# Attention and a routed FFN on one core: the first batch's start reordered, gate halves and threshold moved, and the end behind the last output rearranged

## The chip, the cores and the metric

The kernel runs on one core of a Trainium2 chip. A core has TensorE (PE, with its weight load PEld), VectorE (DVE), ScalarE (ACT), GpSimd (POOL) and SyncE (SP), each with a queue of its own that it works off in order. SBUF is the working memory, PSUM holds what TensorE writes. The metric is the time of one execution on the device, in microseconds; lower is better.

## The reference

For each of eight batches of 3136 tokens (z 64 wide, u and v 256 wide):

```
scores = z z^T / 3136;  attn = max(scores, 0)^2;  x = u * (attn v)
s = x . w_gate;  the 128 tokens with the largest s are chosen
x[chosen] += sigmoid(s) * (relu(x[chosen] w1) w2)        # w1 256 x 1024, w2 1024 x 256
```

The result is x in float32. In the matmuls of attention and FFN each operand is split into a high part (rounded to fp32r) and a low part (the rest), and three of the four products are summed.

## The kernel before

The tokens of a batch are cut into seven chunks of columns (five of 512, one of 256, one of 320; `WHOLE` is 5, `NCH` is 7) and 24 blocks of 128 rows and a half one. A slot is one pair of row blocks against one chunk; a chunk has 13 slots (`SLOTS`), the last with the half block (`n == 1`). Slots are written out in order by the loop at the end, and everything is emitted by hand in that order (`manual_schedule`), so every engine works in the order of the program text.

In a slot k, `mix` (L487) issues PE's matmuls for the slot (`acc`, L517): the high parts, then the low parts. In between, at `turn`, it calls `more_scores(k + LEAD)`, which issues the score matmuls (`sc`, L411) of three slots later and, on ACT, relu (L421) and the square that is rounded to the high part (L422). `settle_scores` then squares on DVE (`a`, L432) and calls `low` (L436), which transposes squares for later use by other chunks (L447), stores them to DRAM, and takes the low part (`lo`, L478) on DVE or POOL, whichever `busy` says has less to do. Scores are symmetric, so later chunks fetch stored squares (`fetch`, `fetch_own`) instead of computing them. A bank of PSUM for scores comes free when DVE has squared it.

`start` (L1199) does the first loads, splits and scores: ten idle matmuls on zeros (`warm`), z and v of the first batch, the split of z into `ZH` and `ZL` and the first chunk's moving operand `Z` (`bring_z`, upper half from ACT, lower from DVE). v is staged in two `vst` buffers, four transfers to a buffer (`stage_v`, L274), and split by `prep_v` (L119 and L120). The same two buffers take the FFN's weights in batch 0 (`load_weight`), which are split into `wh`, `wl` and stored to DRAM (`keep_weight`), and a chunk's own squares (`fetch_own`).

At the end of a chunk, `finish` (L555) multiplies by u (`ut`, L562), transposes x on DVE (`turn`, L573) and stores it (four transfers of 256-byte pieces, L580), and sums the gate. The routing of a batch (`route`: a search for the threshold by eight rounds of count and total, then masks, columns, places, one-hot picks) and its FFN (`expert`: gather by POOL, `hidden`, `turn_h`, `back` to y, scatter by POOL) are lists of tasks, each with PE's operations and a post for the other engines; the loop hands them out to slots of the next batch. In the eighth batch there is no next one: routing starts in its fourth chunk over the first three chunks' tokens (`LATE` is 4), with the gate's 48 columns of runs split into halves by two DVE instructions (`halve`, L653 and L654) to fill more rows, and each later chunk is merged into the choice (`merge`: spread of old scores, counts on DVE, pick, find). A planner in the loop decides by sums of its own (`clock`, `dve_at`, `room`, `ready`) when such a task may go into a slot.

Two FFNs, of batches 5 and 6, are kept (`HELD`, `put_off`) and run behind the last output, beside the last merge (lists f0, s0 of one and f1, s1 of the other; `f` holds the hidden matmuls, the transposes and the first 16 y matmuls, `s` the low parts and the last 8 y and the scatter). Then comes the last batch's own FFN.

```
        late, seen, *rest, find = rest
        run([*rest[: n - 1], f0[0], rest[n - 1], late, seen])
        run([*blend(rest[n:], [*f0[1:], *f1[:2]]), find])
        rest = [*first[:2], *f1[2:], *s0, *s1[:2], *first[3:], *ffn, more[0], *s1[2:], *more[1:]]
```

In the last line `first` is number, gather, nothing, weigh (gate of the chosen, sigmoid) and turn (transpose of the gathered rows and their split).

Of the kernel before, what the change touches and what calls it, by code (L numbers as in the profile page):

```python
# [84 lines left out]
def attention_then_routed_ffn(ctx: ExitStack, tc: tile.TileContext, zt, ut, v, wg, w1, w2, cst, cst16, keys, outs, at, cap):  # L85
# [146 lines left out]
    def prep_z(b, i, of=None):  # L232
# [6 lines left out]
        on = nc.gpsimd.tensor_tensor if b else None  # L239
# [28 lines left out]
    def stage_v(b, g, queue=nc.sync):  # L268

        st = stage.tile([P, GT, D], F32, name="vst", tag="vst")  # L270
        if g < NJ // GT:
            for f in range(GT):
                src = v[b, g * CH + f * P : g * CH + (f + 1) * P, :].rearrange("(t a) d -> a t d", a=Q)
                queue.dma_start(st[f * Q : (f + 1) * Q], src)  # L274
# [5 lines left out]
    def prep_v(b, g, on=None):  # L280
# [10 lines left out]
        if not on and b == 0 and busy["pool"] + 1.3 > busy["dve"] + 0.6:  # L291
            lo_on, took = nc.vector, {"act": 0.6, "dve": 0.6}
# [106 lines left out]
    def scores(k):  # L399
# [9 lines left out]
        for q, j in enumerate(js):  # L409
            for z, start in ((ZH, True), (ZL, False)):  # L410
                nc.tensor.matmul(ps[:, q], z[:, j * P : (j + 1) * P], mov, start=start, stop=not start)  # L411
# [24 lines left out]
    def low(k, a, hi, pieces, square):  # L436
# [5 lines left out]
        rows = slice(0, P) if n == 2 else slice(64, P)  # L442
        if turns(k):
# [36 lines left out]
        else:  # L480
            nc.vector.tensor_tensor(hi[rows], a[rows], hi[rows].bitcast(F32), op=ALU.subtract)
            spend(dve=0.05 + 0.001 * w)
# [4 lines left out]
    def mix(k, beside, between):  # L487
# [24 lines left out]
        turn = (6 if b or c else 3) if first else 4 if last or len(slots[min(k + 1, len(slots) - 1)][2]) == 1 else 8  # L512
# [42 lines left out]
    def finish(b, c):  # L555
# [13 lines left out]
        x = tail.tile([P, CH // Q, NK, Q], F32, name="x", tag="x", bufs=1)[:, :NB]  # L569
# [23 lines left out]

        turns = [lambda h=h: turn(h) for h in range(NK)]
        if scored:
            return [([], turns), ([], [None, add])]
        spread, seen = scores_of(b, c, xT)
        return [(spread, turns), ([], [lambda q=q: seen(q) for q in range(2)])]
# [41 lines left out]
    def route(b):  # L640
# [10 lines left out]
        def halve():  # L651
            whole = gate[b][:, : R // 2]
            nc.vector.tensor_scalar(gate[b][:, R // 2 : R], whole, consts["half"][:, 1:2], None, op0=ALU.mult)  # L653
            nc.vector.tensor_scalar(whole, whole, consts["half"][:, 0:1], None, op0=ALU.mult)  # L654
            spend(dve=0.4)
# [44 lines left out]
        def settle(rd):  # L700
# [7 lines left out]
            base = moe.tile([TP, 1], I32, name="base", tag="base", bufs=2)[:R]  # L708
            if rd == 0:
# [16 lines left out]
        def masks():  # L726
            t = st["base"].bitcast(F32)
            mk = moe.tile([TP, 2 * NT], BF16, name="mk", tag="mk")[:R]
            nc.vector.tensor_scalar(mk[:, :NT], G, t, None, op0=ALU.is_gt)
            nc.vector.tensor_scalar(mk[:, NT:], G, t, None, op0=ALU.is_equal)  # L730
# [218 lines left out]
    def expert(b, st, n):  # L949
# [49 lines left out]
        def bank(name, e):  # L999
            if not roomy:  # L1000
                return misc_bank(name)
            if name == "h" or (not lent and name == "y"):
                return ps_s.tile([P, 2, 512], F32, name=name, tag="sc")[:, 0]
            if lent:
                return ps_a.tile([P, 512], F32, name=name, tag="acc")
            if e == 0:
                st["pair"] = ps_s.tile([P, 2, 512], F32, name=name, tag="sc")
            return st["pair"][:, e]

        def hidden(e, i):  # L1010
            if i == 0:
                st["h", e] = bank("h", e)
# [15 lines left out]
        def turn_h(e, f):  # L1028
            if f == 0:
                st["hT", e] = bank("hT", e)  # L1030
# [22 lines left out]
        def back(i):  # L1053
            if i == 0:
                st["ps"] = bank("y", 0)
# [24 lines left out]
        if roomy:  # L1080
            return first, hid, [tur[0], dif[0], tur[1], dif[1], (to_y, scatter)]
# [17 lines left out]
    for b in range(B):  # L1099
# [18 lines left out]
        for g in range(NJ // 2 + 1):  # L1118
            k = k0 - 10 + 3 * g // 2 if b else max(1, g - 2)
            if b or g > 1:  # L1120
# [78 lines left out]
    def start():  # L1199
        warm(10)  # L1200
# [28 lines left out]
    for k, (b, c, js, is_old) in enumerate(slots):  # L1229
# [8 lines left out]
        if len(js) == 2:  # L1238
            if near and (k % SLOTS or c <= NCH - late if late else k % SLOTS % 3 == 2):
                tasks.append(near.popleft())  # L1240
            if far and far[0] is None and not near and not tasks and not (late and c > NCH - late):
                far.popleft()
                rested = k + 2
            if late and c >= NCH - late:

                left = sum(took_by(i) for i in range(k, k - k % SLOTS + SLOTS))
                room = clock + min(took, left - 3.5)
                asked = 0
                while far and rested <= k and asked < 2 and dve_at + 0.5 * asked < room:
                    if far[0] is None:  # L1250
                        if near:
# [3 lines left out]
                    if far[0][0] and (asked or ready > clock + took):  # L1255
# [16 lines left out]
        if k + 1 < len(slots) and len(slots[k + 1][2]) == 1:  # L1272
# [36 lines left out]
    if merged(B - 1):  # L1309
# [3 lines left out]
        late, seen, *rest, find = rest  # L1313
        n = len(rest) - len(last_merge) + 2
        run([*rest[: n - 1], f0[0], rest[n - 1], late, seen])
        run([*blend(rest[n:], [*f0[1:], *f1[:2]]), find])
        order.enter_context(tc.manual_schedule())
        rest = [*first[:2], *f1[2:], *s0, *s1[:2], *first[3:], *ffn, more[0], *s1[2:], *more[1:]]
# [29 lines left out]
```

## Time and profile before

| | us |
|---|---|
| median of 3 runs (2145.92 to 2148.81) | 2146.33 |
| profiled execution | 2144.29 |
| its span, first to last instruction | 2142.5 |
| TensorE busy | 2105.7 (98%) |
| VectorE busy | 1519.2 (71%) |
| GpSimd busy | 1347.3 (63%) |
| ScalarE busy | 1219.9 (57%) |
| mean granted TensorE clock | 0.995 |

The rows below come from one profiled execution; its time is the span and 1.8 us around it. A view of waits says who waited for whom: us in total, number of waits, longest. A timeline gives start, duration, engine, line, operation, written and read tiles, shape, and in brackets how long the engine had stood idle before and what ended it. Durations of matmuls overlap, so a group's duration holds the last one's drain.

### The profile page before, as it was taken

The page shows a single profiled execution, that of the slowest core. Times are in us where ns is not written, and L with a number is a line of the kernel's source. Part 1 is how long each engine was busy: PE and PEld are TensorE (multiplying, and loading weights), DVE is VectorE, ACT ScalarE, POOL GpSimd, SP SyncE. Part 2 cuts the span into 40 slices and gives each one's busy share as a digit, 9 for nine tenths or more (in the row PEclk, how much of TensorE's full clock was granted, in tenths as well). Part 3 has the DMA queues.
Part 4 walks back from the last instruction along what each step waited for, and adds up shares of the span by engine and source line. Part 5 has one row for each costly group of instructions (what it writes and reads, how often), then busy time and mean ns, then how long its engine had stood idle before and what let it go on. Part 6 is the DMA issues. An engine that isn't in the chain of part 4 may idle for free.

```text
span 2142.5 us, 31762 instructions
## 1 busy us (share of the span) xinstructions
PE 2105.7 (98%) x10575; PEld 1762.2 (82%) x10575; DVE 1519.2 (71%) x2305; ACT 1219.9 (57%) x1488; POOL 1347.3 (63%) x706
## 2 busy tenths in 40 slices
PE   8999999999999999999999999999999999999998
PEld 6778988889888898888988889888888889887787
DVE  7756677765777668776677757776678766877774
ACT  6555476545765457654665546655466554765343
POOL 5765576664766558665586556765576665766543
PEclk9999999999999999999999999999999999999999
DMA  6789666787667876778767777678867687756742
GB/s 173 210 256 228 192 200 176 191 235 217 182 190 191 228 219 189 198 192 224 218 188 207 188 217 225 184 188 193 248 188 207 175 209 190 205 165 184 194 141 79
DMA packets 432948, 422.27 MB, mean 197 GB/s; under 512 B 150160, under 2 KB 341136, under 8 KB 429200
## 3 DMA queue, kind: packets, MB, share of 16 engines
q1 hardware_dynamic: 431440, 417.63, 70.8%
q0 software_dynamic: 768, 2.10, 0.3%
q8 instruction: 83, 1.36, 0.3%
q10 hardware_dynamic: 576, 0.52, 0.1%
q14 instruction: 81, 0.66, 0.1%
HBM read 235.31 MB, written 172.23 MB: 190 GB/s over the span
## 4 chain that ended last, share of the span: by engine, by line
PE 84%; DMA 4%; DVE 3%; issue 3%; ACT 3%; POOL 2%; SPq 1%; POOLq 0%; DVEq 0%; ACTq 0%
PE acc L517 68%; PE sc L411 13%; POOL lo L478 2%; ACT a L421 1%; ACT hi L422 1%; DVE a L432 1%; DMA squares_narrow<-aT 1%; DMA qk<-squares 1%; PE h L1015 1%; PE y L1059 1%; DMA vst<-in_w 1%; DMA ut<-in_ut 0%; SPq L580 0%; DVE beats L871 0%; DVE ut L562 0%
## 5 line engine op out<-in xcount | busy, mean ns | idle before, releaser
L517 PE MATMUL acc<-hi,V 128*128 128x512 f32 (+2 forms) x5376 | 1235.2, 367 | 3.7 <-DVE V L120 2.4
L478 POOL TENSOR_TENSOR lo<-a,hi 128x1024 fp32r<-128x1024 f32 (+2 forms) x327 | 756.4, 2315 | 609.4 <-DVE a L432 503.3
L517 PEld LDWEIGHTS acc<-hi,V 128*128 128x128 f32 x5376 | 935.9, 189 | 169.5 <-DVE ut L562 5.1
L517 PE MATMUL acc<-lo,V 128*128 128x512 f32 (+2 forms) x2688 | 671.6, 366 | 8.4 <-POOL lo L478 8.3
L421 ACT ACTIVATE a<-sc 128x1024 f32<-128x1024 f32 (+4 forms) x408 | 363.2, 890 | 537.4 <-PE sc L411 418.0
L517 PEld LDWEIGHTS acc<-lo,V 128*128 128x128 f32 x2688 | 474.5, 189 | 96.1 <-POOL lo L478 14.2
L432 DVE TENSOR_TENSOR a<-sc,a 128x1024 f32<-128x1024 f32 (+3 forms) x334 | 338.4, 1013 | 278.7 <-ACT hi L422 247.3
L391 ACT CAST hi<-qk 128x1024 fp32r<-128x1024 f32 (+2 forms) x320 | 275.4, 863 | 254.1 <-PE acc L517 200.4
L447 DVE STREAM_TRANSPOSE aT<-a 128x512 f32<-128x512 f32 (+1 forms) x520 | 341.2, 691 | 85.4 <-ACT a L427 53.6
L422 ACT ACTIVATE hi<-a 128x1024 fp32r<-128x1024 f32 (+4 forms) x408 | 377.5, 925 | 17.4 <-PE acc L517 0.2
L478 DVE TENSOR_TENSOR lo<-qk,hi 128x1024 fp32r<-128x1024 f32 (+2 forms) x219 | 292.4, 1342 | 81.6 <-ACT hi L391 76.1
L411 PE MATMUL sc<-Z,ZH 128*128 128x512 f32 (+2 forms) x760 | 283.0, 376 | 4.8 <-DVE Z L256 3.1
L411 PE MATMUL sc<-Z,ZL 128*128 128x512 f32 (+2 forms) x760 | 283.5, 377 | 0.4 <-DVE ZL L120 0.4
L478 POOL TENSOR_TENSOR lo<-qk,hi 128x1024 fp32r<-128x1024 f32 (+2 forms) x101 | 194.1, 1924 | 64.0 <-ACT hi L391 48.5
L411 PEld LDWEIGHTS sc<-Z,ZH 128*128 128x128 f32 x760 | 143.8, 189 | 33.9 <-ACT ZH L119 3.9
L411 PEld LDWEIGHTS sc<-Z,ZL 128*128 128x128 f32 x760 | 143.6, 189 | 26.6 <-DVE ZL L120 0.8
L120 POOL TENSOR_TENSOR V<-vst,V 128x512 fp32r<-128x512 f32 x89 | 122.4, 1380 | 48.0 <-ACT V L119 44.8
L582 POOL TENSOR_TENSOR ut<-x,w_run 128x1024 f32<-128x1024 f32 (+2 forms) x52 | 127.2, 2447 | 25.9 <-DVE x L573 23.9
L119 ACT CAST V<-vst 128x512 fp32r<-128x512 f32 x95 | 57.7, 608 | 39.9 <-DMA vst<-in_v 39.9
L427 ACT ACTIVATE a<-a 128x1024 f32<-128x1024 f32 x74 | 78.5, 1061 | 2.3
L120 POOL TENSOR_TENSOR ZL<-zst,ZH 128x512 fp32r<-128x512 f32 (+2 forms) x56 | 77.9, 1395 | 3.0 <-ACT ZH L119 2.8
L562 DVE SCALAR_TENSOR_TENSOR ut<-acc,ut 128x512 f32<-128x512 f32 (+2 forms) x112 | 64.0, 612 | 19.4 <-PE acc L517 16.4
(148 smaller groups left out, 1045.7 us busy)
## 6 DMA issues: line engine op xcount, KB each, us to landing
squares<-aT SPq DMA_DIRECT2D x160, 512.0 KB, 3.5
qk<-squares SPq DMA_DIRECT2D x320, 256.0 KB, 5.9
squares_narrow<-aT SPq DMA_DIRECT2D x320, 128.0 KB, 3.4
qk<-squares_narrow SPq DMA_DIRECT2D x80, 512.0 KB, 5.0
vst<-in_v SPq DMA_DIRECT2D x188, 128.0 KB, 3.3
ut<-in_ut SPq DMA_DIRECT2D x40, 512.0 KB, 5.4
out<-x SPq DMA_DIRECT2D x160, 128.0 KB, 3.3
squares_own<-aT SPq DMA_DIRECT2D x39, 256.0 KB, 2.1
```

The source lines that it names most:

```text
L120: (lo_on or nc.vector.tensor_tensor)(lo, src, hi.bitcast(F32), op=ALU.subtract)
L391: nc.scalar.copy(by(hi), src)
L411: nc.tensor.matmul(ps[:, q], z[:, j * P : (j + 1) * P], mov, start=start, stop=not start)
L421: nc.scalar.activation(a, ps[:, :n], AF.Relu)
L422: nc.scalar.activation(pieces[0][0](hi), pieces[0][1], AF.Square)
L427: nc.scalar.activation(a, a, AF.Square)
L432: square = lambda: nc.vector.tensor_tensor(a[rows], ps[rows, :n], a[rows], op=ALU.mult)
L447: nc.vector.transpose(to, a[rows, q].rearrange("p (m t a) -> p m t a", t=GT, a=Q))
L478: on.tensor_tensor(view(lo), src, view(hi).bitcast(F32), op=ALU.subtract)
L517: nc.tensor.matmul(ac[h], w, mov, start=first and h not in started, stop=stop)
L562: nc.vector.scalar_tensor_tensor(xT[:, h, :w], acc[b, c][h], SCALE * SCALE, xT[:, h, :w], op0=ALU.mult, op1=ALU.mult)
L582: nc.gpsimd.tensor_tensor(wx, runs, consts["wg_run"].rearrange("p (o r) -> p o r", o=1).broadcast_to([P, NB, RUN]), op=ALU.mult,)
```

## The change

- `start`: twelve idle matmuls instead of ten; the second z load goes ahead of v; two of v's first four transfers go from ACT's queue to SP's; ZL's subtraction for the first block comes behind the lower half of `Z`; both first squares are done before any low part; the split of V's third pair moves here. In the first two score pairs the high parts' matmuls come first.
- `low`: a half block's subtraction (`hi`, L481) comes ahead of its transposes. `mix`: in the first slot of batches 1 to 7, scores are issued after four matmuls, not six.
- Weights of the FFN: loads and splits move from slots 19 to 33 to the second halves of the second and third chunk (loads at 8, 9, 11, 13 of the chunk, splits at 10, 12, 14, 16), and each stored weight follows at slot 17 from that chunk's start.
- `halve` goes to ACT. In the last round of the search the threshold is written to PSUM, and the masks are tensor_tensor with it broadcast, no longer tensor_scalar.
- The planner of the eighth batch: the routing's first task waits a slot more, tasks with matmuls stay out of the first two slots of later chunks, and the last chunk may be filled to 1.5 of its end instead of 3.5.
- Behind the last output x is turned by PE (`flip`, two transposes into a PSUM bank for each 128 tokens), copied by ACT and stored row by row, three transfers. The old scores' spread goes ahead; one kept FFN stands beside the last merge; of the other, the hidden matmuls stand behind the find, the transposes behind the turn, and y in pieces between the last FFN's steps; weigh comes behind the turn. The last y is summed in another order, and banks of PSUM are taken from other pools.

```diff
     def start():
-        warm(10)
+        warm(12)
...
-        stage_v(0, 0, nc.scalar)
         stage_z(0, 1, (WHOLE - 1) * CH, CH)
+        stage_v(0, 0, (nc.scalar, nc.scalar, nc.sync, nc.sync))
...
-        prep_z(0, 0)
+        low_parts = []
+        prep_z(0, 0, on=lambda *x, **how: low_parts.append(lambda: nc.vector.tensor_tensor(*x, **how)))
         bring_z(0, 0)
+        for fn in low_parts:
+            fn()
...
-        settle_scores()
         more_scores(1)
+        square_scores()
         prep_v(0, 1)
         settle_scores()
         prep_z(0, 2, 1)
+        prep_v(0, 2)
...
+        todo = [(q, j, z) for q, j in enumerate(js) for z in (ZH, ZL)]
+        if k < 2:
+            todo.sort(key=lambda x: x[2] is ZL)
...
-        turn = (6 if b or c else 3) if first else 4 if last or ...
+        turn = (6 if c else 4 if b else 3) if first else 4 if last or ...
...
+        def flip(i):
+            h, i = i % NK, i // NK
+            o, n = groups_of(w)[i]
+            if h == 0:
+                flipped.append(ps_a.tile([P, 512], F32, name="flip", tag="acc"))
+            nc.tensor.transpose(flipped[i][:n, h * P : (h + 1) * P], xT[:, h, o : o + n], consts["ident"])
...
-            nc.vector.tensor_scalar(gate[b][:, R // 2 : R], whole, consts["half"][:, 1:2], None, op0=ALU.mult)
-            nc.vector.tensor_scalar(whole, whole, consts["half"][:, 0:1], None, op0=ALU.mult)
+            nc.scalar.mul(gate[b][:, R // 2 : R], whole, consts["half"][:, 1:2])
+            nc.scalar.mul(whole, whole, consts["half"][:, 0:1])
...
+            if rd == last:
+                base = st["ps"][:R, 64:65].bitcast(I32)
...
-            nc.vector.tensor_scalar(mk[:, NT:], G, t, None, op0=ALU.is_equal)
+            nc.vector.tensor_tensor(mk[:, NT:], G, t, op=ALU.is_equal)
...
-        at_slots(SLOTS + 6 + 2 * i, load, use, 0.6)
+        k = (1 + i // 4) * SLOTS
+        loads.append((k + (8, 9, 11, 13)[i % 4], load))
+        at_slot(k + 10 + i % 4 * 2, use, 0.6)
...
-        at_slot(SLOTS + 6 + 8 * i - 1, lambda i=i: keep_weight(i))
+        at_slot(i * SLOTS + 17, lambda i=i: keep_weight(i))
...
-                room = clock + min(took, left - 3.5)
+                room = clock + min(took, left - (3.5 if c < NCH - 1 else 1.5))
...
-                        if near:
+                        if near or (tasks and c == NCH - late):
                             break
...
-                    if far[0][0] and (asked or ready > clock + took):
+                    soon = k % SLOTS < 2 and c > NCH - late
+                    if far[0][0] and (asked or soon or ready > clock + took):
                         break
...
+        out, before, (old, *rest, find) = rest[: len(near)], rest[len(near) : n], rest[n:]
+        spread, seen, *flips = out
+        (ops, post), *f0 = f0
+        run([*before, old, (ops[:3], None), spread, seen, *flips, (ops[3:], post)])
+        run([*blend(rest, f0), find])
...
+        *first, weigh, turn = first
+        to_y = f1.pop()[0]
+        rest = [*first[:2], *f1[:2], *s0, turn, *f1[2:], *s1[:2], weigh, *ffn]
+        rest += [*more[:2], (to_y[:NF], None), *more[2:4], (to_y[NF:], None), *s1[2:], *more[4:]]
```

## Rows read from the trace of the kernel before

**Rows 1.** the page's busy line: busy us, share of the span, instructions

```profile
PE 2105.7 (98%) x10575; PEld 1762.2 (82%) x10575; DVE 1519.2 (71%) x2305; ACT 1219.9 (57%) x1488; POOL 1347.3 (63%) x706
```

**Rows 2.** PE's waits, whole span: us in total, times, longest

```profile
PE acc L517 <- POOL lo L478: 8.3, 12, 2.0
...
PE gate L660 <- DVE gate L654: 2.7, 1, 2.7
...
PE cols L736 <- DVE mk L730: 2.5, 1, 2.5
```

**Rows 3.** stretches: us, busy (instructions) by engine, PEclk granted, DMA, GB/s

```profile
40.00:60.00 20.00, 19.25 (x82) 15.07 (x82) 19.39 (x21) 13.07 (x19) 16.62 (x9) 1.00 0.79 216
...
1980.00:1985.00 5.00, 4.82 (x14) 3.95 (x15) 3.71 (x8) 0.31 (x1) 1.52 (x2) 0.50 1.02 364
...
2017.00:2025.00 8.00, 5.48 (x16) 3.51 (x15) 5.86 (x8) 0.91 (x1) 2.67 (x2) 0.79 0.39 101
...
2127.00:2133.00 6.00, 5.25 (x14) 3.56 (x13) 0.00 (x0) 0.84 (x2) 0.00 (x0) 0.50 0.00 0
```

**Rows 4.** timeline of the start

```profile
1.20 4.45 PE L1197 MATMUL idle<-zero 128*128 128x512 bf16 x10 [1.20 <-DVE zero L1194]
...
3.90 2.58 ACTq L274 DMA_DIRECT2D vst<-in_v  x2
...
8.71 0.77 PE L411 MATMUL sc<-Z,ZH 128*128 128x512 f32 x1 [3.06 <-DVE Z L256]
...
12.96 1.38 PE L517 MATMUL acc<-hi,V 128*128 128x512 f32 x3
...
16.61 0.50 PE L411 MATMUL sc<-Z,ZH 128*128 128x512 f32 x1 [1.19 <-DVE a L432]
...
26.17 2.27 PE L517 MATMUL acc<-hi,V 128*128 128x512 f32 x7 [2.37 <-DVE V L120]
```

**Rows 5.** waits of ACT and PE from 100 to 150 us

```profile
ACT wh L119 <- DMA vst<-in_w: 13.8, 4, 6.8
ACT wh L119 <- DMA w1h_there<-wh: 5.5, 1, 5.5
...
PE acc L517 <- POOL lo L478: 3.6, 3, 2.0
```

**Rows 6.** timeline of the eighth batch's halving and mask

```profile
1977.76 2.33 POOL L478 TENSOR_TENSOR lo<-qk,hi 128x1024 fp32r<-128x1024 f32 x1
1977.87 2.25 DVE L654 TENSOR_SCALAR gate<-gate,c_sb 128x48 f32<-128x48 f32 x1
...
2017.34 2.36 DVE L730 TENSOR_SCALAR mk<-G,base 96x16 bf16<-96x16 f32 x1
```

**Rows 7.** DVE's groups by shape: count | busy us, mean ns | idle before

```profile
L432 DVE TENSOR_TENSOR a<-sc,a 128x1024 f32<-128x1024 f32 x207 | 252.9, 1222 | 236.1 <-ACT hi L422 206.1 <-issue 16.0 <-POOL wl L120 9.5
...
L120 DVE TENSOR_TENSOR V<-vst,V 128x512 fp32r<-128x512 f32 x7 | 8.6, 1244 | 0.0
...
L730 DVE TENSOR_SCALAR mk<-G,base 98x32 bf16<-98x32 f32 x7 | 1.6, 232 | 0.0
```

**Rows 8.** timeline behind the last output

```profile
2111.38 0.90 DVE L573 STREAM_TRANSPOSE x<-ut 128x320 f32<-128x320 f32 x2
...
2116.75 0.69 DVE L921 SCALAR_TENSOR_TENSOR oh<-rk,c_sb 128x512 bf16<-128x512 f32 x1
...
2118.69 0.31 PE L937 MATMUL ids<-c,oh 128*128 128x2 bf16 x3
...
2119.57 1.02 POOL L968 DMA_INDIRECT xe<-out,ids  x1 [14.52 <-DVE ids L960]
...
2122.64 1.11 PE L1059 MATMUL y<-ZH,hl 128*128 128x256 f32 x8
...
2126.36 0.92 PE L1015 MATMUL h<-wh,xh 128*128 128x512 f32 x2 [2.39 <-ACT xh L119]
...
2137.84 0.48 DVE L1065 SCALAR_TENSOR_TENSOR y<-y,g,xe 128x256 f32<-128x256 f32 x1 [1.52 <-PE y L1059]
```

More of the change, by code (lines that the diff above doesn't have):

```diff
@@ L290, in prep_v @@
         lo_on, took = on or nc.gpsimd, {"dve": 1.0} if on else {"act": 0.6, "pool": 1.3}
-        if not on and b == 0 and busy["pool"] + 1.3 > busy["dve"] + 0.6:
+        if not on and b == 0 and n == 2 and busy["pool"] + 1.3 > busy["dve"] + 0.6:
             lo_on, took = nc.vector, {"act": 0.6, "dve": 0.6}
@@ L408, in scores @@
         ps = ps_s.tile([P, 2, CH], F32, name="sc", tag="sc")[:, :, :w]
[L409 to L411 removed]
+        todo = [(q, j, z) for q, j in enumerate(js) for z in (ZH, ZL)]
+        if k < 2:
+            todo.sort(key=lambda x: x[2] is ZL)
+        for q, j, z in todo:
+            nc.tensor.matmul(ps[:, q], z[:, j * P : (j + 1) * P], mov, start=z is ZH, stop=z is ZL)
         a = work.tile([P, 2, CH], F32, name="a", tag="a")[:, :n, :w]
@@ L511, in mix @@
                 todo.sort(key=lambda x: x[0])
-        turn = (6 if b or c else 3) if first else 4 if last or len(slots[min(k + 1, len(slots) - 1)][2]) == 1 else 8
+        turn = (6 if c else 4 if b else 3) if first else 4 if last or len(slots[min(k + 1, len(slots) - 1)][2]) == 1 else 8
         done, lead, started = 0, 2, set()
@@ L597, in finish @@
         spread, seen = scores_of(b, c, xT)
+        if c == NCH - 1:
+            flips = [([lambda i=i, h=h: flip(i * NK + h) for h in range(NK)], lambda i=i: store(i)) for i in range(-(-w // P))]
+            return [(spread, None), ([], [lambda q=q: seen(q) for q in range(2)]), *flips]
         return [(spread, turns), ([], [lambda q=q: seen(q) for q in range(2)])]
@@ L997, in turned, with bank @@
             st.update(xh=xh, xl=xl)
-        def bank(name, e):
+        def bank(name):
             if not roomy:
                 return misc_bank(name)
-            if name == "h" or (not lent and name == "y"):
+            if name == "h":
                 return ps_s.tile([P, 2, 512], F32, name=name, tag="sc")[:, 0]
[L1004 to L1008, printed above, removed]
+            if name == "y" and b == B - 1:
+                return misc_bank(name)
+            return ps_a.tile([P, 512], F32, name=name, tag="acc")
         def hidden(e, i):
             if i == 0:
-                st["h", e] = bank("h", e)
+                st["h", e] = bank("h")
             w1h, w1l = (w.rearrange("p (k f) -> p k f", k=NK) for w in w_here)
@@ L1029, in turn_h @@
             if f == 0:
[L1030 removed]
+                st["hT", e] = bank("hT")
             nc.tensor.transpose(
@@ L1240, in attention_then_routed_ffn @@
                 tasks.append(near.popleft())
-            if far and far[0] is None and not near and not tasks and not (late and c > NCH - late):
+            if far and far[0] is None and not near and not tasks and not (late and c >= NCH - late):
                 far.popleft()
@@ L1271, in attention_then_routed_ffn @@
         held_posts = []
-        if k + 1 < len(slots) and len(slots[k + 1][2]) == 1:
+        if k + 2 < len(slots) and len(slots[k + 1][2]) == 1:
             now = square_scores if c < WHOLE and (b or c) else settle_scores
@@ L1312, in attention_then_routed_ffn @@
         (f0, s0), (f1, s1) = held
[L1313 to L1316, printed above, removed]
+        n = len(rest) - len(last_merge)
+        out, before, (old, *rest, find) = rest[: len(near)], rest[len(near) : n], rest[n:]
[3 more added lines that the diff above has]
+        run([*blend(rest, f0), find])
         order.enter_context(tc.manual_schedule())
-        rest = [*first[:2], *f1[2:], *s0, *s1[:2], *first[3:], *ffn, more[0], *s1[2:], *more[1:]]
+        *first, weigh, turn = first
+        to_y = f1.pop()[0]
+        rest = [*first[:2], *f1[:2], *s0, turn, *f1[2:], *s1[:2], weigh, *ffn]
+        rest += [*more[:2], (to_y[:NF], None), *more[2:4], (to_y[NF:], None), *s1[2:], *more[4:]]
     run(rest)
```

35 lines of the change are left out of this document (22 added, 13 removed).

## The prediction

> **What bounds the kernel now.** The page's busy line comes first: TensorE (PE) is busy for 2105.7 of 2142.5 us, and no other engine passes 71% (PEld is PE's own weight load) [rows 1]. So time can only be won where PE stands still (36.8 us in all) or runs at half clock, and a faster VectorE (DVE), ScalarE (ACT) or GpSimd (POOL) counts only where PE waits for it. The list of PE's waits is second [rows 2]. Apart from the two ends it has two large single waits, both in the eighth batch: 2.7 us before the matmul that folds the gate, and 2.5 us before the one that counts columns. The third row is a sum of twelve waits for low parts, 8.3 us. Third come stretches with the granted clock [rows 3]: at 1980 us and at 2127 us it is 0.50, the 1.2 GHz level, each time right behind a standstill of PE. Last comes the timeline of both ends [rows 4, 8], where single waits of 1 to 3 us follow each other.
>
> **A, the start.** Ten idle matmuls run from 1.20 us for 4.45 us, 0.44 each, and the first score matmul comes at 8.71, having waited 3.06 us for DVE's half of Z [rows 4]. ACT's first split stands behind ACT's own queue, which issues its last two v transfers from 3.90 to 6.48. The change gives these two to SP, and on DVE puts the half of Z ahead of ZL. The score can then not start before the twelve idle matmuls end, at 1.2 + 12 x 0.44 = 6.5. If the split gains nothing, only one 0.7 us subtraction goes out of the way, and the score starts at 8.0. I take 6.5, since the split's data were asked for before ACT's v; gain 2.2 (0.7 to 2.2). From the score to the first acc (12.96) the chain over ACT stays the same, and with the first pair's high parts sorted ahead it waits less for ZL. On SP the two transfers push back the next four v and four z transfers by two issues, 2.6 us at most (ACT's own two took 2.58); that data is for later blocks, so I cost it at nothing, and if that cover is gone at 1.3, half of it.
> Two more waits go. The 1.19 us at 16.61 is a score waiting for DVE's square of the second pair; DVE did a low part in between, and both squares now come first. The 2.37 us at 26.17 is the third pair of V, whose split now is in the start. Behind it seven matmuls take 2.27 us, 0.32 each against 0.23 at full clock (below): 0.6 more. Together 2.2 + 1.2 + 2.4 + 0.6 = 6.4. What is late next is DVE: it is busy for 19.39 of 20 us from 40 to 60 [rows 3], so PE can't stay ahead of it by all of that, and the split of V's second pair, which POOL did, falls to DVE by the planner's sums. I take 4.5 (bounds 0.7 and 6.4).
>
> **B, weights of the FFN in batch 0.** They are split in slots 19 to 33 now, and share the two vst buffers with the chunk's own squares. ACT waits in order for four of these transfers, 13.8 us together, and once 5.5 us until a finished weight has been stored to DRAM [rows 5]. Behind ACT wait the scores, then POOL's low parts, and in this stretch PE stands for 3.6 us. The change puts four loads in the second half of each of two chunks, when the chunk's own squares have been taken, with one slot more of lead for three of them, and keeps the first weight two slots ahead of what overwrites it. If all is well 3.6 us go. The load isn't smaller, only later, and the second store falls into the next chunk's fetches of squares; no row shows that collision, so I bound it by this stretch's own 3.6 us, turned round. I take 2.5 (-3.6 to 3.6).
>
> **Middle batches.** Scores come two matmuls earlier in one slot of each of seven batches: 7 x 2 x 0.23 = 3.3 us at most either way, and likely nothing, as 8.3 us of waits for low parts are all that could shrink; I take 0.5 (-2 to 2). The half rows' subtraction goes ahead of its transposes, same work; it is hidden by PE's other matmuls, and if that cover is gone the transposes' 0.7 us is the price: 0.
>
> **C, the eighth batch.** The second half of the gate's halving takes DVE 2.25 us, beside a POOL instruction of 2.33 us that began 0.11 us before [rows 6]. PE, having waited 2.7, is then busy for 4.82 of 5 us at a granted clock of 0.50 [rows 3], half of which, 2.4, full clock would save: 5.1 together. ACT gets the two instructions; between the 0.23 us of a small mask [rows 7] and DVE's own 2.25 each, they are hidden, for the planner now starts routing a slot later than the sum they need, and a slot is over 2.8 us of PE (12 x 0.234, below). Behind them on ACT wait the scores of four slots later. The mask's second half shows the same: 2.36 us, seven others of its kind 0.23 on average [rows 6, 7]; PE's wait of 2.5, and behind it 5.48 us busy at a mean of 0.79, of which 1.2 is the clock's: 3.7. Its new form reads the threshold from PSUM. DVE's square, one input from PSUM and one from SBUF, has a mean of 1.22 us over 207 [rows 7]. Reading the new mask by that row it takes its 0.23 each, and PE's wait ends. At the worst, nothing changes for it: 0.
> The Trainium skill ("SBUF — State Buffer", Who interferes with whom) says that DVE's tensor_scalar can enter a mode that takes the port pair shared with GpSimd, that whoever comes second waits until the other has finished, and that an instruction with at most one SBUF input outside of these modes doesn't contend. The trace agrees for the halving, whose 2.25 us end with POOL's 2.33. By it the 3.7 are certain, without it they are 0 to 3.7.
> Against these 8.8 stands the planner's new order: routing starts a slot later and no task with matmuls runs in the first two slots of a chunk, so everything behind it is later by one to three slots; new waits of the kind just removed can come. I charge 1.8: 7 (0 to 8.8).
>
> **D, behind the last output.** DVE's chain to the last choice holds the two transposes of x, 0.90 us [rows 8], which go to PE and ACT. Three of the six kept hidden matmuls that PE did ahead of this chain's input come behind it, 0.7 at most, of which I take 0.4: 1.3. The pick ends at 2117.44, but PE comes to the find at 2118.69, behind kept hidden matmuls: 1.2 more, of which 0.6 goes, since only one kept FFN stands before it now. The six new transposes on PE and three copies on ACT lie beside DVE's counting (5.2 us up to the pick); I price a transpose as a y matmul, 0.12, a copy at most at DVE's 0.45 for as many columns. Behind the copies wait the kept FFN's relus; without that cover the find is 1.4 later. The gather, at 2119.57 now, comes 1.9 sooner.
> From gather to the first hidden matmul it is 6.79 us (to 2126.36), of which PE stands 2.39, behind a split that ACT does only after the gate (weigh). Now the turn is ahead of weigh, and twelve hidden matmuls, eight y and eight transposes stand in between: 2.8 + 0.9 + 1.0 = 4.7, begun about 0.5 us before the gather, and the turn's 0.2. So 4.4, a gain of 2.4.
> From there to the last y takes 11.48 us now (to 2137.84), half of it at a clock of 0.50 [rows 3, 8]. The row of y has eight in 1.11 us, the last one's drain of 0.17 included: 0.117 for 256 columns, 0.234 for 512. At full clock: twelve hidden 2.8, eight transposes 1.0, a wait for ACT 0.3, and now 24 kept y beside 24 own, 5.6: 9.7, and 0.3 of drain. Gain 1.5. If the clock falls all the same, hidden matmuls cost 2.8 more, and it is -1.3. Sum 1.9 + 2.4 + 1.5 = 5.8 (2.5 to 7).
>
> **Sum.** 4.5 + 2.5 + 0.5 + 7 + 5.8 = 20.3 us. The profiled execution took 2144.29 us (1.79 around its span), 2.0 below the median shown, so 2124.0 for it, and 2126 against the median of 2146.33.
>
> **Rivals.**
> 1. DVE becomes the bound in the first chunk, and the start's gain is given back until 66 us. For it: 97% busy from 40 to 60. Against it: its work hangs on PE's scores and would start sooner with them. The low parts of V moved to DVE have two inputs in SBUF; seven such took 1.24 us on average [rows 7], and one that meets POOL as the mask did costs 2.1 more. A gives 1: 2129.5. The Trainium skill (same page and section) has a DVE instruction with two SBUF inputs contend with a POOL one that reads SBUF; by it the 1.24 is that wait, and this rival is the likelier for it.
> 2. The later routing leaves the merge of the sixth chunk unfinished at the last output, and it stands ahead of the last merge. Its DVE work is about what the last one has between the transposes' end (2112.3) and the pick (2117.44), 5.2, and an exchange with PE, about 7; the hidden matmuls fall to half clock, 2.8. 2126 + 10 = 2136. For it: two of thirteen slots in each late chunk are barred. Against: in the last chunk the planner may now fill slots up to 1.5 instead of 3.5 us of its end.
> 3. The weights' second store and loads collide with fetches of squares in the fourth chunk: B is -3.6, 2132.
> 4. Slower: two merges are left over, 14 us of DVE with PE nearly idle, so that the whole tail runs at 0.50, 12 x 0.234 + 48 x 0.117 = 8.4 more; with C at 4 instead of 7, 2126 + 14 + 8.4 + 3 = 2151. It decides from 20 us of added tail on.
>
> **How the numbers follow.** Forecast 0.60, rival 1 0.15, rival 2 0.10, rival 3 0.08, rival 4 0.04, and 0.03 that the mask and halving change nothing and PE's waits stay (2136 or more). The measurement tells 0.2% (4.3 us) from no change: faster means below 2142.0. The forecast and rivals 1 and 3 are faster, rival 2 for most of its width; same 0.07, slower 0.05. The forecast's own range is 2117 to 2134; with the rivals' times and the bounds of A to D, 2114 to 2140.
>
> **What would show it.** Right: the first score near 6.5 and no wait for V near 21 to 26; no wait of 2 us or more before the fold and cols, and no stretch at 0.50 behind them; ACT without waits for the weights; the gather 1.9 us nearer to the last ut; hidden matmuls of the last FFN 0.23 apart; no DVE transposes in the tail. Wrong: a row of counting (beats) of the sixth chunk behind the last output, DVE above 98% and PE waiting for it before 66 us, ACT's hi waiting for fetched squares from 150 to 200 us, or the hidden matmuls of the last FFN 0.43 apart.

## The result and the profile after

The changed kernel takes 2116.31 us (median of 4 runs, 2114.85 to 2118.16) against 2146.42 (4 runs) for the kernel before in the same comparison. The ratio is 0.9858, with a 95% interval of 0.9841 to 0.9875: 30 us, 1.4%. The forecast was 2126 in a range of 2114 to 2140. The profiled execution took 2115.92, its span is 2114.1, 28.4 us shorter than before; the forecast for a gain in the profile was 20.3.

The busy line of the changed kernel's page:

```profile
PE 2095.5 (99%) x10583; PEld 1754.7 (83%) x10583; DVE 1520.9 (72%) x2304; ACT 1221.6 (58%) x1493; POOL 1345.6 (64%) x703
```

Against [rows 1] PE stands still for 18.6 us instead of 36.8, 18.2 less, and is busy for 10.2 less, with eight more instructions: fewer matmuls run at half clock (the mean granted clock is 1.000, 0.995 before). PE's waits over the whole span (us in total, times, longest):

```profile
PE acc L519 <- POOL lo L483: 3.1, 3, 1.9
PE sc L413 <- DVE a L434: 2.4, 4, 0.8
PE xeT L1011 <- DMA xe<-out,ids: 1.3, 1, 1.3
...
PE sc L413 <- DVE Z L256: 1.0, 1, 1.0
```

The waits before the fold and before the columns [rows 2] are gone; low parts cost 3.1 us instead of 8.3. Stretches of the eighth batch (us, busy by engine, clock, DMA, GB/s) have no standstill and no fallen clock, where [rows 3] had 0.50 and 0.79:

```profile
1970.00:1975.00 5.00, 5.00 (x27) 4.02 (x25) 3.08 (x7) 1.94 (x3) 5.00 (x3) 1.00 1.05 335
...
2017.00:2025.00 8.00, 8.00 (x37) 6.42 (x36) 5.69 (x11) 2.42 (x3) 4.91 (x3) 1.00 0.65 152
```

To see where time was won, I mark in each trace the instant at which DVE begins the output rows (`ut`) of each chunk, and call the difference from the profile of before the lead. It is a difference from one profile; how far profiles of the same code lie apart is told with e3 and e4. It is 6.6 us at the end of the first chunk, 7.35 after the second, 10.0 after the fourth, 8.5 after the first chunk of the second batch, 9.2 after the third chunk of the last batch. Then the fourth chunk adds 5.9, the fifth 5.8, the sixth 1.1, the seventh 0.3 (22.3), and what follows the last mark 6.0 (28.4).

The start, which answers to [rows 4] (start, duration, and in brackets the idle time before with its releaser):

```profile
1.20 4.38 PE L1224 MATMUL idle<-zero 128*128 128x512 bf16 x12 [1.20 <-DVE zero L1221]
6.59 0.71 PE L413 MATMUL sc<-Z,ZH 128*128 128x512 f32 x2 [1.01 <-DVE Z L256]
...
10.16 0.97 PE L519 MATMUL acc<-hi,V 128*128 128x512 f32 x3 [0.82 <-ACT hi L424]
...
13.43 0.50 PE L413 MATMUL sc<-Z,ZH 128*128 128x512 f32 x1 [0.80 <-DVE a L434]
```

The end, which answers to [rows 8]:

```profile
2086.03 0.89 DVE L564 SCALAR_TENSOR_TENSOR ut<-acc,ut 128x320 f32<-128x320 f32 x2 [0.33 <-PE acc L519]
...
2088.93 0.29 DVE L653 SCALAR_TENSOR_TENSOR own<-spread,c_sb 128x128 f32<-128x128 f32 x1 [1.29 <-ACT row L647]
...
2093.28 0.69 DVE L945 SCALAR_TENSOR_TENSOR oh<-rk,c_sb 128x512 bf16<-128x512 f32 x1
...
2095.45 1.02 POOL L992 DMA_INDIRECT xe<-out,ids  x1 [11.68 <-DVE ids L984]
...
2099.68 0.71 PE L1037 MATMUL h<-wh,xh 128*128 128x512 f32 x2
...
2109.47 0.48 DVE L1087 SCALAR_TENSOR_TENSOR y<-y,g,xe 128x256 f32<-128x256 f32 x1 [2.24 <-PE y L1081]
```

From the last `ut` to the gather it is 9.42 us (11.22 before), from there to the first own hidden matmul 4.23 (6.79), and to the last y 9.79 (11.48).

### The profile page after: what moved, and what is told of

It is laid out like the page before. It is cut to its first block, busy times and chain, and to the rows that moved or that the text cites. A ratio compares the mean times of both kernels' runs of the same rounds, so it can differ in the third digit from the quotient of the medians.

```text
span 2114.1 us, 31795 instructions
## 1 busy us (share of the span) xinstructions
PE 2095.5 (99%) x10583; PEld 1754.7 (83%) x10583; DVE 1520.9 (72%) x2304; ACT 1221.6 (58%) x1493; POOL 1345.6 (64%) x703
## 4 chain that ended last, share of the span: by engine, by line
PE 87%; DMA 3%; DVE 2%; issue 2%; ACT 2%; POOL 2%; SPq 1%; POOLq 0%; DVEq 0%; ACTq 0%
PE acc L519 71%; PE sc L413 14%; POOL lo L483 1%; ACT a L423 1%; ACT hi L424 1%; PE h L1037 1%; DVE a L434 1%; DMA qk<-squares_narrow 1%; PE y L1081 1%; DMA qk<-squares 0%; DMA squares<-aT 0%; DVE lo L483 0%; SPq L381 0%; DVE ut L564 0%; SPq L466 0%
## 5 line engine op out<-in xcount | busy, mean ns | idle before, releaser
L483 DVE TENSOR_TENSOR lo<-qk,hi 128x1024 fp32r<-128x1024 f32 (+2 forms) x223 | 299.5, 1350 | 72.1 <-ACT hi L391 69.6
L483 POOL TENSOR_TENSOR lo<-qk,hi 128x1024 fp32r<-128x1024 f32 (+2 forms) x97 | 188.8, 1950 | 57.7 <-ACT hi L391 39.1
```

The lines of the kernel that those rows point to most:

```text
L483: on.tensor_tensor(view(lo), src, view(hi).bitcast(F32), op=ALU.subtract)
```

## The experiments

Length of the last batch's fourth to seventh chunk between marks, in us, for the kernels below:

| kernel | fourth | fifth | sixth | seventh | sum |
|---|---|---|---|---|---|
| before | 46.76 | 45.92 | 23.01 | 24.59 | 140.3 |
| e3, start alone (this batch as before) | 43.73 | 47.20 | 23.01 | 24.59 | 138.5 |
| e4, weights alone (this batch as before) | 45.72 | 45.91 | 23.01 | 24.59 | 139.2 |
| e6, masks as tensor_tensor, threshold in SBUF | 45.68 | 42.10 | 24.54 | 24.59 | 136.9 |
| e1, new forms alone | 41.03 | 41.68 | 24.56 | 24.59 | 131.9 |
| e7, routing a slot later alone | 41.84 | 42.59 | 24.56 | 24.59 | 133.6 |
| e2, whole new order alone | 41.86 | 41.91 | 21.89 | 24.29 | 130.0 |
| u1, changed, old forms back | 41.87 | 40.10 | 21.89 | 24.32 | 128.2 |
| changed | 40.88 | 40.09 | 21.89 | 24.29 | 127.2 |
| changed, once more | 40.92 | 40.06 | 21.89 | 24.31 | 127.2 |

**e1: the forms alone.** In the kernel before, halving on ACT and masks with the threshold in PSUM:

```diff
-            nc.vector.tensor_scalar(gate[b][:, R // 2 : R], whole, consts["half"][:, 1:2], None, op0=ALU.mult)
+            nc.scalar.mul(gate[b][:, R // 2 : R], whole, consts["half"][:, 1:2])
...
+            if rd == last:
+                base = st["ps"][:R, 64:65].bitcast(I32)
...
-            nc.vector.tensor_scalar(mk[:, :NT], G, t, None, op0=ALU.is_gt)
+            nc.vector.tensor_tensor(mk[:, :NT], G, t, op=ALU.is_gt)
```

> The kernel before with the new forms of two steps alone: the gate is halved by ScalarE and the masks read the threshold from PSUM with tensor_tensor; the order is that of before. Theory, forms: both stalls of the eighth batch are meetings of one form of a VectorE instruction with a GpSimd one, so the fold has no wait of 2 us, the masks take 0.2 us each, the lead over before grows by 5 to 6 us in the fourth chunk and 3.7 or more in the fifth, 9 to 12 together: about 2135. Rival, order: PE only comes to the next wait sooner, a wait of 1 us or more stays before the fold or the columns, and the lead is under 4 us: 2142 or more.

Measured: 2137.72 us, ratio 0.9958 (0.9942 to 0.9975); both waits gone; the lead grew by 5.7 in the fourth and 4.2 in the fifth chunk, and 1.6 of that was given back in the sixth. The first theory's rows hold, with 8.4 us below its 9 to 12. The timeline of POOL and DVE around the masks:

```profile
2011.37 2.40 POOL L478 TENSOR_TENSOR lo<-a,hi 128x1024 fp32r<-128x1024 f32 x1 [2.77 <-DVE a L432]
...
2013.05 0.17 DVE L731 TENSOR_TENSOR mk<-G,tot 96x16 bf16<-96x16 f32 x1
2013.13 0.16 DVE L732 TENSOR_TENSOR mk<-G,tot 96x16 bf16<-96x16 f32 x1
```

Both masks ran inside POOL's instruction, which worked until 2013.77, and took 0.17 and 0.16. The Trainium skill ("SBUF — State Buffer", Who interferes with whom) has a DVE instruction with at most one SBUF input, outside the modes that take the second port pair, run beside GpSimd undisturbed; these two rows agree.

**e2: the order alone.** The planner's four new rules in the kernel before, halving and masks untouched:

```diff
-            if far and far[0] is None and not near and not tasks and not (late and c > NCH - late):
+            if far and far[0] is None and not near and not tasks and not (late and c >= NCH - late):
...
-                room = clock + min(took, left - 3.5)
+                room = clock + min(took, left - (3.5 if c < NCH - 1 else 1.5))
...
-                        if near:
+                        if near or (tasks and c == NCH - late):
...
-                    if far[0][0] and (asked or ready > clock + took):
+                    soon = k % SLOTS < 2 and c > NCH - late
+                    if far[0][0] and (asked or soon or ready > clock + took):
```

> The kernel before with the planner's new order in the late chunks alone (routing a slot later, no task with matmuls in the first two slots of a chunk, slots filled up to 1.5 us of the last chunk's end). Theory, forms: the halving and the second mask still meet GpSimd and take over 2 us, and the order itself costs 0 to 2 us: 2144 to 2149. Rival, order: the stalls go because the work behind them moves; PE's waits before fold and columns shrink under 1 us, and the lead over before at the end of the last batch is 9 us or more: about 2136. Between them (a lead of 2 to 8 us): both have a share.

Measured: 2139.17 us, ratio 0.9967 (0.9955 to 0.998); 10.3 us won in the four chunks, more than the forms alone in these traces. The timed ratios, 7.1 us (4.3 to 9.7) and 9.0 (5.4 to 12.4) for e1, do not tell the two apart; behind the last mark e2 takes 0.6 longer than before. The rival is right on the waits and on the four chunks, and the time lies between its 2136 and the theory's 2144. The halving still meets POOL, and the fold doesn't wait (no idle time in brackets); the masks, now twelve us later, fell clear of POOL and took 0.23 each in their old form:

```profile
1982.53 2.43 POOL L478 TENSOR_TENSOR lo<-qk,hi 128x1024 fp32r<-128x1024 f32 x1
...
1982.67 2.33 DVE L654 TENSOR_SCALAR gate<-gate,c_sb 128x48 f32<-128x48 f32 x1
...
1985.06 0.51 PE L660 MATMUL gate<-c_sb,gate 128*96 128x16 f32 x4
```

**e7: two of the four rules**, the first and the third of that diff, by which routing and merging start only in a slot without another task.

> The kernel before with two of the four rules of the new order alone: routing and merging may start only in a slot without another task. Theory: the one slot is what decides, since it puts the halving ahead of a slot that PE can fill and the masks where GpSimd is idle; leads of 4 to 5 us in the fourth and 3 to 4 us in the fifth chunk of the last batch, as with all four rules; masks of 0.23 us; about 2139. Rival, the bar on matmuls in the first two slots of a chunk decides: the fold still waits for 1 us or more, or the leads together are under 5 us; 2142 or more.

Measured: 2136.74 us, ratio 0.9957 (0.9941 to 0.9974); leads of 4.9 and 3.3 in the fourth and fifth chunk, as the theory has it, but not for its reason: the second mask still met POOL.

```profile
2015.17 2.43 DVE L730 TENSOR_SCALAR mk<-G,base 96x16 bf16<-96x16 f32 x1
...
2018.96 0.22 PE L736 MATMUL cols<-c,mk 96*32 96x96 bf16 x1
```

PE came to `cols` behind other matmuls and did not wait. So the delay stays, and cover takes its cost away. The sixth chunk's 1.6 us are lost as in e1. e2, which also has the bar on matmuls in a chunk's first two slots, wins 1.1 there: the bar is worth 2.7 us in this chunk (e2's fourth rule, the closer end, counts in the last chunk alone).

**u1: the changed kernel with the old forms back** (e1's edit undone, the order kept).

> The changed kernel with halving and masks back in the old forms on VectorE, everything else as changed. Theory, order has a share of its own: GpSimd is idle where the masks stand now, so they take 0.23 us each; the halving meets a low part and takes 1 to 3.4 us, of which the fold waits for 0 to 2; the fourth to the seventh chunk of the last batch lose 0 to 3 us against the changed kernel: 2116 to 2119. Rival, forms are additive: they lose the 8.4 us that the forms alone won: 2125.

Measured: 2116.77 us, ratio 0.9865 (0.9848 to 0.9882), against 0.9862 (0.9845 to 0.9878) for the changed kernel in the same comparison: no difference that can be measured. In the trace it is 1.0 us, all in the fourth chunk. The halving takes 2.33 us again and PE comes to the fold 0.06 after its end:

```profile
1967.57 2.33 DVE L676 TENSOR_SCALAR gate<-gate,c_sb 128x48 f32<-128x48 f32 x1
...
1969.96 0.51 PE L682 MATMUL gate<-c_sb,gate 128*96 128x16 f32 x4
```

The masks are 0.23 each, as POOL is idle there. Forms (8.4 alone) and order (10.3 alone) remove the same stalls; the changed kernel, which has both and more, wins 13.1 and not 18.7. What is left from e2 to u1, 1.8 in the fifth chunk, is where e2 still had a wait of 1.8 us for `ut` that u1 hasn't; the edits that could do it (half rows' subtraction ahead of the transposes, the last slots' posts) were not run by themselves.

**e6: the masks as tensor_tensor, the threshold left in SBUF**, in the kernel before.

> The kernel before with the masks as tensor_tensor, but with the threshold still in SBUF (two inputs from SBUF). GpSimd works without a gap around them, as before. Theory, PSUM counts: an instruction with two SBUF inputs still meets GpSimd, the second mask takes over 1 us or both together over 1.5 us (3.1 before), and PE's wait before the columns stays above 1 us. Rival, the form counts: tensor_scalar alone is slow, the masks take 0.2 us each and PE's wait before the columns is gone.

Measured: one time, 2144.75 us; PE's wait before the columns 0.3. The fifth chunk is 3.8 us shorter, of which 1.5 are given back in the sixth. POOL and DVE around the masks:

```profile
2017.78 2.39 POOL L478 TENSOR_TENSOR lo<-a,hi 128x1024 fp32r<-128x1024 f32 x1 [2.76 <-DVE a L432]
2020.14 2.41 POOL L478 TENSOR_TENSOR lo<-qk,hi 128x1024 fp32r<-128x1024 f32 x1
```

```profile
2019.45 0.76 DVE L729 TENSOR_TENSOR mk<-G,base 96x16 bf16<-96x16 f32 x1
2020.13 0.16 DVE L730 TENSOR_TENSOR mk<-G,base 96x16 bf16<-96x16 f32 x1
```

The first mask in the kernel before, and POOL at the second mask of [rows 6]:

```profile
2016.66 0.76 DVE L729 TENSOR_SCALAR mk<-G,base 96x16 bf16<-96x16 f32 x1
...
2017.35 2.32 POOL L478 TENSOR_TENSOR lo<-qk,hi 128x1024 fp32r<-128x1024 f32 x1
```

Each theory is right for one mask. The first, two inputs from SBUF beside a POOL instruction that already runs, takes 0.76 as in the old form and ends with that instruction, at 2020.2; so PSUM has a part in e1's 0.17. The second begins 0.01 us before POOL's next instruction in both kernels; the old form took 2.36 there, the new one 0.16. For that one the form was enough. The new form was seen there once; the old one took 2.36 to 2.43 at such a place in four profiles (before, e3, e4, e7).

**e3 and e4: the start alone, the weights alone**, in the kernel before. The core of e3:

```diff
-        warm(10)
+        warm(12)
...
-        stage_v(0, 0, nc.scalar)
+        stage_v(0, 0, (nc.scalar, nc.scalar, nc.sync, nc.sync))
...
+        square_scores()
...
+        prep_v(0, 2)
```

and of e4:

```diff
-        at_slots(SLOTS + 6 + 2 * i, load, use, 0.6)
+        k = (1 + i // 4) * SLOTS
+        loads.append((k + (8, 9, 11, 13)[i % 4], load))
+        at_slot(k + 10 + i % 4 * 2, use, 0.6)
```

> The kernel before with the start's edits alone (queues, order of splits, twelve idle matmuls, third V pair in the start). Theory: the lead over before is 6.6 us at the end of the first chunk, as it was in the whole change, and stays to the end: about 2140. Rival, VectorE bound: without the weights' edits the lead is given back, under 4 us from the second chunk on, 2143 or more.

> The kernel before with the FFN weights' loads, splits and stores at their new slots alone. Theory: ScalarE's waits for weight transfers (13.8 and 5.5 us) go and so does PE's 3.6 us behind them by the fourth chunk; about 1 us is given back before the second batch: lead 2 to 3.6 us, about 2143. Rival, no gain of its own: the lead is under 1 us at the second batch, and the 3 us that the changed kernel won between its first and fourth chunk came from the start's edits: 2146.

Measured: e3 2140.02 us, ratio 0.9978 (0.9968 to 0.9988); e4 2142.08 us, 0.998 (0.997 to 0.9989). Leads: e3 6.55, 7.3, then 5.0 at the second batch and about 4 from the fourth on; e4 0.2, 2.3 after the fourth chunk, 1.5 at the second batch, 0.0 ahead of the last batch's fourth chunk. Against their theories both leads are right early and leak later, but the leads are against one profile, and that profile was a quick one in the first batch: in four profiles with start and weights as before (e1, e2, e6, e7) the first mark of the second batch came 1.7 to 4.1 us later than in it. The timed ratios don't have this fault: 4.7 us (2.6 to 6.9) and 4.3 (2.4 to 6.4). ScalarE's waits for weight transfers are not all gone: 6.1 us in two waits in the changed kernel, for 13.8 and 5.5 [rows 5].

These two traces also show the eighth batch's stall with nothing changed there. Stretches behind the fold's wait, e3 first, then e4 and e6, which has this wait too:

```profile
1975.00:1980.00 5.00, 3.81 (x20) 3.15 (x21) 4.26 (x8) 1.05 (x1) 1.83 (x2) 1.00 0.98 316
```

```profile
1980.00:1985.00 5.00, 4.81 (x18) 3.79 (x18) 3.71 (x8) 1.04 (x1) 1.83 (x2) 0.67 1.00 336
```

```profile
1985.00:1990.00 5.00, 5.00 (x17) 3.92 (x16) 4.04 (x11) 1.05 (x1) 2.88 (x2) 0.67 0.98 378
```

The same wait of 2.7 us stands ahead of all three, as of [rows 3] at 0.50. The fourth chunk took 43.73 us in e3, 45.72 in e4, 45.68 in e6, 46.76 before. So of the 5.9 us that the changed kernel won there, 1 to 3 hung on what the clock did in that one execution. In the fifth chunk e3 was the slow one. With the code of before the four chunks took 138.5 to 140.3 us, so the changed kernel's gain in them is 11.4 to 13.1, and the other gains in the table have as much play.

**r1: the changed kernel once more.**

> The changed kernel once more, unchanged. If the 13.1 us of the eighth batch are the change's own, the marks of its last batch repeat within 1 us and so does the first chunk's 6.6 us; differences of up to 2 us between marks elsewhere would show how much a single profile can tell. About 2116.

Measured: 2116.61 us, ratio 0.9862 (0.9845 to 0.9878). The first mark's lead is 6.98 (6.58), the four chunks are the same within 0.04 each, and what follows the last mark within 0.02; in the first batch the leads differ by up to 1.1.

**u4: weigh ahead of turn again**, in the changed kernel:

```diff
-        rest = [*first[:2], *f1[:2], *s0, turn, *f1[2:], *s1[:2], weigh, *ffn]
+        rest = [*first[:2], *f1[:2], *s0, weigh, turn, *f1[2:], *s1[:2], *ffn]
```

> The changed kernel with one move undone in the tail: the gate of the last FFN is weighed ahead of the turn of its input, as before. Theory: ScalarE's split waits for the gate, the first hidden matmul of the last FFN comes 0.7 to 2.4 us later after the gather (4.2 in the changed kernel) and the last y as much later: 2117 to 2119. Rival, the kept FFN's matmuls cover the gate: under 0.5 us.

Measured: 2117.55 us, ratio 0.9877 (0.986 to 0.9893). ACT's gate, its split and PE:

```profile
2098.00 0.20 ACT L1001 ACTIVATE g<-ge 128x1 f32<-128x1 f32 x1 [1.15 <-DVE junk L546]
2098.11 0.35 ACT L119 CAST xh<-xeT 128x256 fp32r<-128x256 f32 x1
```

```profile
2096.95 0.38 PE L1011 MATMUL xeT<-c_sb,xe 128*128 128x128 f32 x2
2098.52 0.73 PE L1037 MATMUL h<-wh,xh 128*128 128x512 f32 x2 [0.32 <-ACT xh L119]
```

From gather to own hidden matmuls it is 4.79 us, 0.56 more, and the end comes 0.3 later. The rival, nearly: the split still follows the gate, but kept matmuls fill the time.

**u5: x of the last chunk turned by DVE again**, in the changed kernel (the branch for the last chunk in `finish` never taken).

> The changed kernel with x of the last chunk turned by VectorE again (two transposes of 0.45 us), and without the six transposes of TensorE and three copies of ScalarE. Theory: the transposes stand in VectorE's chain to the last choice, the gather comes 0.9 us later behind the last output's first row and so does the end: about 2117.5. Rival: the chain has 0.9 us to spare or the transposes are covered, under 0.3 us. It could also be sooner, if the copies on ScalarE hold up the relus of the kept FFN: then by up to 1 us.

Measured: 2117.05 us, ratio 0.987 (0.9853 to 0.9886). DVE behind the last output:

```profile
2084.74 0.89 DVE L564 SCALAR_TENSOR_TENSOR ut<-acc,ut 128x320 f32<-128x320 f32 x2 [0.33 <-PE acc L519]
...
2086.27 0.90 DVE L576 STREAM_TRANSPOSE x<-ut 128x320 f32<-128x320 f32 x2
...
2087.66 0.29 DVE L653 SCALAR_TENSOR_TENSOR own<-spread,c_sb 128x128 f32<-128x128 f32 x1 [0.48 <-ACT row L647]
```

`own` begins 2.92 us after `ut`, 2.90 in the changed kernel, where DVE waits 1.29 for ACT's `row` instead of 0.48. The transposes lie in that gap: the rival, 0. This holds for PE's new order. In the kernel before, ACT's `row` and `own` stand so:

```profile
2111.35 0.43 ACT L625 COPY row<-spread 128x320 f32<-128x320 f32 x1 [0.55 <-PE spread L621]
...
2112.40 0.29 DVE L631 SCALAR_TENSOR_TENSOR own<-spread,c_sb 128x128 f32<-128x128 f32 x1
```

There `row` was done at 2111.78 and the transposes of [rows 8] at 2112.28, so they did hold `own` up, by 0.6 us at most; no run took them away alone.

**v1 and v2: a version that might be better.** In the changed kernel PE's longest wait, 1.9 us at 63 us, is for a low part; behind it stands ACT's wait of 4.1 us for the last half V block. v1 splits that block a slot later, v2 also gives its low part to DVE (only the edit that both have is shown):

```diff
-                at_slot(k, lambda b=b, g=g: prep_v(b, g))
+                at_slot(k + (1 if b == 0 and 2 * g == NJ else 0), lambda b=b, g=g: prep_v(b, g))
```

> The changed kernel with the split of the first batch's last half V block one slot later, so that ScalarE's wait of 4.1 us for its transfer no longer stands ahead of the scores of the second chunk. Theory: PE's wait of 1.9 us for the low part at 63 us shrinks below 0.7, the mark of the first chunk's end is the same within 0.5 and the next one 1 to 2.5 us sooner; 2113 to 2115. Rival: the V block itself comes late, PE waits for Vr by 1 us or more at the first chunk's end and nothing is won: 2116 or more.

> As the version with the last half V block split one slot later, and its low part on VectorE instead of GpSimd, where it stood behind a low part of the scores and came 3.6 us late. Theory: no wait for Vr, PE's wait of 1.6 to 1.9 us for the low part at 63 us shrinks below 0.7, the lead over before at the second mark is 8.5 to 10 us (7.4 and 8.2 in two profiles of the changed kernel); 2114 to 2116. Rival: VectorE is late with its squares in turn and PE waits for a score's square by 1 us or more: no gain, 2116 or more.

Measured: v1 2120.37 us, ratio 0.9877 (0.9861 to 0.9894); v2 2117.36, 0.9871 (0.9854 to 0.9887); leads at the second mark 4.0 and 5.9 (7.4 and 8.2 in the changed kernel). PE's waits in the first 150 us, v1, then v2:

```profile
PE acc L519 <- POOL Vr L120: 3.6, 1, 3.6
```

```profile
PE acc L519 <- DVE Vr L120: 2.7, 1, 2.7
```

In v1 the block stands behind a low part on POOL; in v2 behind two DVE transposes that wait 1.7 and 0.8 us for stores. The wait moved to where the block is needed. No version here beats the changed kernel.

## Why the prediction was right, and where its working was not

**Right in direction and range**, 10 us too slow. The profile of before was quick in the first batch, so each term is also given by means: over the profiles in which its stretch is as before, less those in which it is as changed (six and six for A, five and five for B with the middle batches, three and six for C, seven and five for D). By these A is worth 6.2 us, B with the middle batches 6.0, C 12.2 and D 5.8, together 30.2; the timed medians differ by 30.1. So C is half of the miss, B with the middle batches 3 us of it and A 2.

**A, the start**: 4.5 forecast, with an upper bound of 6.4. Measured are 6.6 at the first mark (6.5 to 7.0 in six profiles with this start), and 6.2 by the means, as six profiles with the old start lie 1.7 apart there. The wait for V of 2.37 went; the one of 1.19 for DVE's square is still 0.80, at 13.43. The first score came at 6.59, where 6.5 was taken, but that is luck: the idle matmuls, which were to set it, ended at 5.58, and the score waited 1.01 more for DVE's half of `Z`. The sum also took the way from there to the first `acc` as unchanged. It is 3.57 us instead of 4.25, as the score matmuls follow each other faster: the first eight take 2.15 instead of 3.55. The two us held back for DVE were not needed: from 40 to 60 us it is busy for 16.58 instead of 19.39 [rows 3].

**B and the middle batches**: 2.5 + 0.5 forecast, 2.6 against the profile of before, which was the quickest of five with this code in the stretch, by 1.9 to 5.3 us. By the means it is 5.8 in the rest of the first batch and 0.2 in the batches behind it; by e4's timed ratio the weights are worth 4.3 (2.4 to 6.4). So B was priced too low, by these means beyond its bound of 3.6. The mechanism holds, with a third of ACT's waits left. PE stands still for 4.0 us less and is busy for 2.0 less in the stretch; no run tells what these are made of.

**C, the eighth batch, is the step that failed in size**: 7 (0 to 8.8) forecast, 13.1 measured, 12.2 by the means. Its terms were 5.1 + 3.7 for the stalls and -1.8 for the planner's order. The stalls' 8.8 was right: e1 alone gives 8.4. The charge had the wrong sign: the order alone wins 10.3, since PE's other matmuls cover the halving (e2) and the second mask (e7). The forms are worth their 8.4 only alone; with the new order in place they give 1.0 (u1), so either edit removes most of the stalls.

The sum also left out the waits for half rows, which come third in the view of [rows 2]:

```profile
PE acc L517 <- DVE hi L481: 2.9, 2, 1.8
```

The prediction put the half rows' subtraction at 0, as hidden by PE's other matmuls. The 2.9 us fall into the fifth and sixth chunk of the last batch and are as long in e1; in the changed kernel both are gone, and one of 0.5 stands in the last chunk. By their rows DVE meets POOL here too. First the subtraction in the sixth chunk before, with POOL beside it, then the same one in the changed kernel, where POOL is idle (in the fifth chunk they take 1.66 and 0.69):

```profile
2079.91 4.61 POOL L478 TENSOR_TENSOR lo<-qk,hi 128x512 fp32r<-128x512 f32 x3
...
2081.97 1.13 DVE L481 TENSOR_TENSOR hi<-a,hi 64x256 fp32r<-64x256 f32 x1
```

```profile
2059.69 0.42 DVE L446 TENSOR_TENSOR hi<-a,hi 64x256 fp32r<-64x256 f32 x1
```

In e2, without the subtraction's edit, they are gone as well, and a wait of 1.8 for `ut` came instead; which edit does how much of this is open.

**D, the tail**: 5.8 forecast, 6.0 measured (5.8 by the means), its three parts 1.80 (1.9), 2.56 (2.4) and 1.69 (1.5). But inside the first part two errors cancel, which is luck. It had 0.9 for the transposes, 0.4 for PE's order and 0.6 for the find. With PE's new order the transposes are worth nothing (u5); `oh` comes 7.25 us after `ut` instead of 8.40, and by elimination the 1.15 between them are PE's order, with `old` and `spread` ahead of kept matmuls; no run tried it alone. The find gave 0.65. Of the second part, turn ahead of weigh carries 0.3 to 0.6 (u4); the rest came with the new order of the kept work, which no run took apart. The third hangs on the clock of one execution: from the last FFN's first hidden matmul to the last y it is 11.47 or 11.48 in six of seven profiles with the old tail, and 10.03 in e4 (mean granted clock 0.84 there, 0.70 before).

**The rivals** did not come: DVE did not bind the first chunk (a V split on DVE that met POOL took 2.26 us where the one before took 0.65, but one took 2.27 in the kernel before too), no merge was left over, and the weights' second store cost nothing that the marks show.

## What to carry to other kernels

A stall can be cured by a faster instruction or by work put in front of the one that waits; find out which of two edits does it by undoing each in the changed kernel, for gains of 8.4 and 10.3 us, with further edits, made 13.1 together, and the new forms could be dropped again for 1.0. Before an instruction is moved to another engine, look at the idle time behind it on its own, in the order in which it is going to run: DVE's transposes would have lain in a wait of 1.3 us. And list every wait of the stage with the engine that ends it: the 2.9 us for half rows stood beside the two stalls that I priced.

## What was not expected of the hardware

The same wait of 2.7 us before the fold was followed by five microseconds at a granted clock of 0.50, 0.67, 0.67 and 1.00 in four profiles of the same instructions (before, e4, e6, e3), and the chunk took 46.76, 45.72, 45.68 and 43.73 us. What half clock costs behind such a standstill differed from execution to execution, and a single profile shows one of the cases; no run shows what decides it.
